# Turning k by a DMA transpose of two 16-bit planes in a recurrence-and-GLU kernel, from the seventh chunk on

## The chip, the cores and the metric

One NeuronCore of one Trainium2 chip runs the kernel in one launch. The metric is the device time of one execution in microseconds, as the median of three runs; beside it stands one execution that the hardware profiler recorded, and all rows below are of that one. The engines are named as the profile names them: PE is TensorE's matmul (PEld its weight load), DVE is VectorE, ACT is ScalarE, POOL is GpSimd, SP is the sync engine, which issues nearly all DMAs here.

## What is computed

A linear recurrence with a decay for each channel, over 4 batches, 8 heads and 768 steps with head size 48, and then a gated linear unit on its 3072 outputs of width 384.

```python
for t in range(S):                                   # per batch and head
    cur = np.einsum('bhd,bhe->bhde', u[None] * kt, vt)
    y[:, :, t] = np.einsum('bhd,bhde->bhe', rt, state + cur)
    state = wt[:, :, :, None] * state + np.einsum('bhd,bhe->bhde', kt, vt)
...
g = x @ w_gate                                       # x: [3072, 384], w_gate: [384, 1536]
silu = g * (1.0 / (1.0 + np.exp(-g)))
val = x @ w_val
return (silu * val @ w_out).astype(np.float32)
```

## The kernel before

The steps are cut into 24 chunks of 128, numbered so that chunk n belongs to batch n mod 4. A chunk's k and r come as one tile `kr` with channels on 112 partitions (two heads of 48 with 16 empty ones between) and four head pairs times 128 steps beside each other. Two scans on DVE (`scan`, `scan2`) run along the decays; `kq` and `re` multiply k and r with them. Within a chunk the recurrence is then three kinds of matmul: `sc` gives the scores of k against r, `dl` the chunk's contribution to the state from k and v, and `y` or, from chunk 6 on, `yy` the outputs from scores, v and state. `dl` needs k with the steps on partitions. `kb` makes it with four TensorE transposes for each chunk into a PSUM buffer (tag `pa`, two buffers, shared with `sc` and `yy`), and `kn` copies that buffer to SBUF on ACT.

From chunk 6 on (`PAIRED = 6`) two chunks n and n + 1 go together through `sc`, `dl` and `yy`, with chunks of 64 steps inside. Their outputs pass through ACT (`xp`), ten small DMAs on SP that move them to the layout of the GLU (`xd`), and a split into a high and a low part (`xh` on ACT, `xl` on DVE).

The GLU runs over seven groups of 4, 2, 4, 4, 4, 4 and 2 chunks' outputs (`GROUPS`). For each group and each of 12 blocks f of 128 hidden channels there are two sets of nine matmuls, `gv` with j = 0 and 1 (PSUM, two buffers), then `silu` (ACT, reads j = 0), `sg` (DVE, multiplies with j = 1), `hh` (ACT) and `hl` (DVE), which split the product, and `po`, three matmuls for each tile of 128 outputs. All products use a high and a low part, hence three matmuls for one. The weights are loaded and split into the two parts during the first group (`raw` to `lower`).

The order of all this is one table, `ORDER`, whose items are run through a dictionary of functions; an item `gv:2:5:1` is group 2, block 5, j = 1, and `kn:13` is kn of chunk 13. Each engine, and SP's queue of DMAs, executes its own instructions in the order of the table, and waits where data or a buffer is missing. `nat` (k and r with steps on partitions, loaded for the diagonal: `ru`, `ruk` and `a0` on DVE use it) lives in a tag with one buffer, `at` in one with three:

```python
nats[n] = ld.tile([P, 2, H, D], F32, tag="nat", name=f"nat_{n}", bufs=1)
...
ats[n, j] = a = ap_.tile([P, 2, NPR, HALF], F32, tag="at", name=f"at_{n}_{j}", bufs=3)
...
for item in ORDER.split():
    name, *at = item.split(":")
    ops[name](*(int(a) if a.isdigit() else a for a in at))
```

Of the kernel before, what the change touches and what calls it, by code (L numbers as in the profile page):

```python
# [70 lines left out]
gv:0:8:1 gv:0:8:0 half spb:5 hh:0:7 pred:5:1 upper:9 y:5 hl:0:7 top:10 xh:5 lower:9 scan:6 kr:7 dl:5  # L71
silu:0:8 low:10 top:11 vt:7 shift:10 po:0:7 low:11 sign:10 sg:0:8 plus:10 hh:0:8 whole:6 a0:6 gv:0:9:1
gv:0:9:0 kr:6 upper:10 hl:0:8 lower:10 po:0:8 xm:5 silu:0:9 sg:0:9 shift:11 sign:11 gv:0:10:0 hh:0:9
nat:7 plus:11 upper:11 hl:0:9 gv:0:10:1 po:0:9 kq:6 silu:0:10 lower:11 sg:0:10 seed:6 scan2:6 vt:6
# [5 lines left out]
hh:1:2 check2:4 vt:8 po:1:1 gv:1:3:0 hl:1:2 silu:1:3 gv:1:3:1 sc:6 sg:1:3 re:8 dl:6 hh:1:3 hl:1:3 st1:6  # L80
st1:7 zs:7:1 ruk:8 ws2:2 ws:9 st2:6 po:1:2 ob:0:3 out:0:3 gv:1:4:0 zero:8 check2:2 st2:7 silu:1:4 scan:9
gv:1:4:1 own:6:0 seed:9 sg:1:4 ob:0:1 zs:7:0 hh:1:4 a0:8 po:1:3 gv:1:5:0 rc:7 pred:6:1 whole:9 zs:6:1
hl:1:4 gv:1:5:1 nat:9 silu:1:5 pred:6:0 sg:1:5 yy:6 kr:10 sps:8 ru:9 gv:1:6:0 kq:9 hh:1:5 gv:1:6:1
po:1:4 scan2:9 hl:1:5 silu:1:6 xp:6:1 sps:9 sg:1:6 ruk:9 hh:1:6 ws:10 hl:1:6 gv:1:7:0 re:9 xp:6:0 zero:9
po:1:5 gv:1:7:1 a0:9 scan:10 silu:1:7 seed:10 sg:1:7 gv:1:8:0 kb:8 nat:10 kb:9 kq:10 ws2:5 hh:1:7
gv:1:8:1 whole:10 hl:1:7 zs:8:0 kn:9 scan2:10 kn:8 po:1:6 silu:1:8 sg:1:8 rc:9 gv:1:9:0 check2:5 hh:1:8
ru:10 gv:1:9:1 out:0:2 own:8:0 sc:8 out:0:1 own:8:1 hl:1:8 xd:6 silu:1:9 ruk:10 sg:1:9 dl:8 st1:8 kr:11
xh:6 st1:9 pred:8:0 po:1:7 hh:1:9 gv:1:10:0 vt:10 pred:8:1 a0:10 st2:8 zs:9:1 zs:8:1 rc:8 st2:9 vt:11
zs:9:0 hl:1:9 yy:8 silu:1:10 nat:11 zero:10 gv:1:10:1 xp:8:1 sg:1:10 re:10 ws:11 ws:12 scan:11 po:1:8
gv:1:11:1 xp:8:0 hh:1:10 whole:11 hl:1:10 kq:11 po:1:9 gv:1:11:0 silu:1:11 kb:11 kb:10 xd:8 ru:11 xl:6  # L90
sg:1:11 hh:1:11 ruk:11 xh:8 hl:1:11 po:1:10 xl:8 po:1:11:c1 kn:10 sps:11 po:1:11:c0 a0:11 seed:11
zs:11:0 scan2:11 gv:2:0:0 gv:2:0:1 re:11 nat:12 ru:12 silu:2:0 zero:11 kr:12 own:10:0 gv:2:1:1 sg:2:0
gv:2:1:0 hh:2:0 scan:12 ob:1:0 seed:12 hl:2:0 silu:2:1 po:2:0:c2 whole:12 sg:2:1 own:10:1 rc:11
po:2:0:c3 kq:12 hh:2:1 gv:2:2:1 gv:2:2:0 scan2:12 ob:1:1 ruk:12 ws2:6 hl:2:1 po:2:0:c0 kn:11 sps:10
check:12 silu:2:2 kr:13 po:2:0:c1 re:12 sc:10 sg:2:2 dl:10 pred:10:0 zero:12 ws:13 st1:10 a0:12 check2:6
st1:11 po:2:1 pred:10:1 vt:12 nat:13 gv:2:3:0 scan:13 hh:2:2 st2:10 st2:11 hl:2:2 vt:13 po:2:2 silu:2:3
ru:13 ruk:13 gv:2:3:1 a0:13 rc:10 zs:10:0 sg:2:3 zs:11:1 gv:2:4:0 gv:2:4:1 seed:13 out:1:1 nat:14 hh:2:3
whole:13 hl:2:3 silu:2:4 gv:2:5:1 zs:10:1 kq:13 sg:2:4 scan2:13 yy:10 xp:10:1 ws:14 ru:14 hh:2:4 hl:2:4
sps:12 kr:14 zero:13 xp:10:0 gv:2:5:0 st2:20 silu:2:5 ruk:14 po:2:3 sg:2:5 kr:15 re:13 gv:2:6:0 hh:2:5
hl:2:5 scan:14 kb:12 kb:13 silu:2:6 gv:2:6:1 sg:2:6 po:2:4 hh:2:6 a0:14 hl:2:6 xd:10 kq:14 gv:2:7:0  # L100
sps:13 whole:14 gv:2:7:1 kn:13 seed:14 silu:2:7 scan2:14 kn:12 sg:2:7 own:12:0 re:14 nat:15 sc:12
check:13 dl:12 po:2:5 st1:12 zero:14 own:12:1 vt:15 st1:13 ws:15 zs:12:0 scan:15 pred:12:0 gv:2:8:0
hh:2:7 kq:15 st2:12 pred:12:1 seed:15 check:14 st2:13 po:2:6 rc:13 ws:16 ru:15 st2:21 whole:15 hl:2:7
po:2:7 ruk:15 gv:2:8:1 zs:13:0 zs:12:1 scan2:15 silu:2:8 re:15 gv:2:9:0 check:15 xh:10 sg:2:8 hh:2:8
ws2:1 zs:13:1 rc:12 hl:2:8 yy:12 sps:14 gv:2:9:1 rc:14 a0:15 silu:2:9 po:2:8 kr:17 out:1:0 own:14:1
xp:12:0 gv:2:10:0 zero:15 check2:1 zs:14:0 sg:2:9 hh:2:9 hl:2:9 gv:2:10:1 vt:17 xp:12:1 xd:12 kr:16
silu:2:10 xh:12 sg:2:10 hh:2:10 scan:16 xl:10 hl:2:10 gv:2:11:1 nat:16 xl:12 gv:2:11:0 kb:14 kb:15 ru:16
po:2:9 own:14:0 silu:2:11 gv:3:0:0 sg:2:11 kn:15 seed:16 sps:15 vt:14 kn:14 hh:2:11 po:2:10 ruk:16
hl:2:11 silu:3:0 vt:16 ws2:3 sc:14 dl:14 po:2:11:c0 st1:14 whole:16 ob:2:0 st1:15 kq:16 po:2:11:c3
st2:14 st2:15 po:2:11:c1 gv:3:0:1 sg:3:0 scan2:16 gv:3:1:0 hh:3:0 po:2:11:c2 check2:3 hl:3:0 a0:16  # L110
out:2:0 ob:2:2 zs:14:1 silu:3:1 pred:14:1 gv:3:1:1 ob:2:1 sg:3:1 re:16 po:3:0:c3 gv:3:2:0 hh:3:1 rc:15
nat:17 po:3:0:c0 zero:16 hl:3:1 out:2:2 gv:3:2:1 po:3:0:c1 ws:17 zs:15:0 ob:2:3 silu:3:2 pred:14:0
zs:15:1 po:3:0:c2 sg:3:2 ru:17 hh:3:2 gv:3:3:0 hl:3:2 po:3:1 yy:14 ruk:17 rc:16 xp:14:0 silu:3:3
gv:3:3:1 gv:3:4:0 sps:16 scan:17 check:16 sg:3:3 gv:3:4:1 a0:17 nat:18 whole:17 po:3:2 ru:18 hh:3:3
hl:3:3 silu:3:4 sg:3:4 hh:3:4 gv:3:5:1 own:16:0 seed:17 ruk:18 hl:3:4 gv:3:5:0 po:3:3 a0:18 kq:17 ws:18
kb:16 xp:14:1 scan2:17 silu:3:5 kb:17 own:16:1 nat:19 gv:3:6:0 vt:19 re:17 sg:3:5 hh:3:5 zero:17
gv:3:6:1 kr:18 po:3:4 hl:3:5 xd:14 silu:3:6 sg:3:6 po:3:5 hh:3:6 kn:17 kn:16 rc:17 gv:3:7:0 scan:18
kq:18 check:17 hl:3:6 whole:18 silu:3:7 sc:16 out:2:3 dl:16 seed:18 sps:17 scan2:18 st1:16 ru:19 st1:17
zs:16:1 zs:17:1 pred:16:1 ws:19 zero:18 re:18 po:3:6 check:18 st2:16 zs:16:0 ws2:8 st2:17 gv:3:7:1
# [842 lines left out]
```

## Time and profile before

| | |
|---|---|
| median of three runs | 562.36 us (560.94 to 563.23) |
| the profiled execution, its own time | 560.63 us |
| its span, first to last instruction | 558.9 us |
| PE busy, share of the span | 545.6 us, 98% |
| DVE busy | 326.1 us, 58% |
| ACT busy | 260.1 us, 47% |
| DMA traffic | 54.64 MB, mean 98 GB/s |

Busy time is counted between the first start and the last end of overlapping instructions. A matmul's end is modelled, and matmuls overlap, so the price of one on TensorE is read from the start of one to the start of the next. The page's chain follows the work that ended last backwards from the end; the timeline lists instructions in order of time with idle time in brackets; the windows give the busy time of each engine by stage.

### The profile page before, as it was taken

Reading aid. Unit: us, or ns where it says so; the run is one execution under the profiler, and the core shown is the slowest. Engines: PE = TensorE matmul, PEld = TensorE weight load, DVE = VectorE, ACT = ScalarE, POOL = GpSimd, SP = SyncE. Lnnn points to the kernel's source line nnn. Section 1 sums busy time; section 2 is a strip of 40 time slices with the busy share of each in tenths; the row PEclk is TensorE's granted clock in tenths of the full one; section 3 lists DMA queues with packets and bytes.
Section 4 is the critical chain, followed back from the end, with each engine's and each line's share of the span. In section 5 each row is a group of like instructions: output and inputs, shape, how many; then the busy total and the mean of one; then the engine's idle time right before and its main releaser. Section 6 shows DMA issues by size and latency. Waiting matters only on the chain.

```text
span 558.9 us, 12807 instructions
## 1 busy us (share of the span) xinstructions
PE 545.6 (98%) x5406; PEld 478.0 (86%) x5406; DVE 326.1 (58%) x523; ACT 260.1 (47%) x535; POOL 4.8 (1%) x36
## 2 busy tenths in 40 slices
...
GB/s 249 276 168 212 129 193 167 225 43 162 103 205 75 109 103 104 68 90 125 74 48 114 71 51 89 42 109 31 113 10 71 87 36 0 1 25 22 15 32 61
DMA packets 28494, 54.64 MB, mean 98 GB/s; under 512 B 4176, under 2 KB 14800, under 8 KB 28432
## 3 DMA queue, kind: packets, MB, share of 16 engines
...
q14 instruction: 18, 0.15, 0.1%
q10 hardware_dynamic: 160, 0.10, 0.1%
...
## 4 chain that ended last, share of the span: by engine, by line
PE 88%; DMA 5%; DVE 2%; SPq 2%; ACT 1%; issue 1%; ACTq 0%; DVEq 0%
PE gv L733 51%; PE po L772 26%; DMA kr<-in_kr_dram 4%; PE y L658 3%; PE sc L516 2%; PE dl L594 2%; PE kb L483 1%; SPq L690 1%; PE y L634 1%; DMA ws<-in_wt_dram 1%; PE sc L505 1%; PE gv_0b L733 0%; PE gv_1b L733 0%; DMA x<-late 0%; SPq L287 0%
## 5 line engine op out<-in xcount | busy, mean ns | idle before, releaser
L733 PE MATMUL gv<-x,w_h 128*128 128x512 f32 (+1 forms) x984 | 285.2, 362 | 2.7 <-ACT x L699 1.7
L733 PEld LDWEIGHTS gv<-x,w_h 128*128 128x128 f32 x984 | 176.6, 188 | 32.9 <-ACT x L699 2.0
L733 PE MATMUL gv<-x,w_l 128*128 128x512 f32 (+1 forms) x492 | 176.8, 359 | 0.0
L746 DVE TENSOR_TENSOR sg<-sg,gv 128x512 f32<-128x512 f32 (+1 forms) x82 | 49.9, 608 | 136.0 <-PE gv L733 101.7
L733 PEld LDWEIGHTS gv<-x,w_l 128*128 128x128 f32 x492 | 92.4, 188 | 12.0
L751 ACT ACTIVATE hh<-sg 128x512 fp32r<-128x512 f32 (+1 forms) x82 | 46.6, 568 | 112.4 <-DVE sg L746 72.1
L772 PE MATMUL po<-w_h,hh 128*128 128x384 f32 x280 | 96.1, 343 | 0.0
L772 PE MATMUL po<-w_h,hl 128*128 128x384 f32 x280 | 94.7, 338 | 0.0
L772 PE MATMUL po<-w_l,hh 128*128 128x384 f32 x280 | 94.1, 336 | 0.0
L743 ACT ACTIVATE sg<-gv 128x512 f32<-128x512 f32 (+1 forms) x82 | 43.7, 532 | 86.7 <-PE gv L733 63.9
L756 DVE TENSOR_TENSOR hl<-sg,hh 128x512 fp32r<-128x512 f32 (+1 forms) x82 | 50.1, 611 | 45.7 <-ACT hh L751 45.0
L772 PEld LDWEIGHTS po<-w_h,hh 128*128 128x128 f32 x280 | 52.5, 188 | 2.9 <-ACT hh L751 0.4
L772 PEld LDWEIGHTS po<-w_h,hl 128*128 128x128 f32 x280 | 52.5, 188 | 2.7 <-DVE hl L756 0.7
L772 PEld LDWEIGHTS po<-w_l,hh 128*128 128x128 f32 x280 | 52.5, 188 | 0.0
L403 DVE TENSOR_TENSOR_SCAN qt<-ws,d 112x516 f32<-112x516 f32 x24 | 29.5, 1228 | 3.8 <-DMA ws<-in_wt_dram 3.8
L419 DVE TENSOR_TENSOR_SCAN et<-ws,d 112x516 f32<-112x516 f32 x24 | 29.5, 1230 | 3.1 <-ACT pend L408 2.3
L794 ACT ACTIVATE ob<-po 128x384 f32<-128x384 f32 x23 | 11.2, 485 | 16.2 <-PE po L772 13.8
L576 ACT ACTIVATE vz<-late 48x192 f32<-48x192 f32 x36 | 12.9, 361 | 10.7 <-DVE late L607 9.3
L434 ACT ACTIVATE ws<-ws,w_top 112x517 f32<-112x517 f32 x24 | 17.5, 730 | 0.8
L315 ACT ACTIVATE w_h<-s 128x1152 fp32r<-128x1152 f32 x12 | 13.9, 1162 | 7.7 <-DVE s L312 7.7
L294 ACT ACTIVATE raw<-raw 128x1152 f32<-128x1152 f32 x12 | 15.4, 1287 | 3.2 <-issue 1.6
L679 ACT ACTIVATE late<-y 112x512 f32<-112x512 f32 x18 | 10.3, 590 | 13.9 <-PE y L658 13.9
...
## 6 DMA issues: line engine op xcount, KB each, us to landing
...
ws<-in_wt_dram SPq DMA_DIRECT2D x36, 226.2 KB, 3.4
kr<-in_kr_dram SPq DMA_DIRECT2D x16, 448.0 KB, 5.5
...
late<-in_kr_dram SPq DMA_DIRECT2D x8, 448.0 KB, 5.0
...
```

The source lines that it names most:

```text
L294: keep(nc.scalar.activation(t, t, AF.Copy, scale=2.0**-112))
L315: keep(nc.scalar.activation(w_h[:, f], ints[f].bitcast(F32), AF.Copy))
L403: keep(nc.vector.tensor_tensor_scan(_flat(qts[n])[:, ::-1], wss[n][:, 1:][:, ::-1], _flat(d1)[:, ::-1], 0.0, ALU.mult, ALU.add))
L419: keep(nc.vector.tensor_tensor_scan(_flat(ets[n]), wss[n][:, :L], _flat(d1), 0.0, ALU.mult, ALU.add))
L434: keep(nc.scalar.activation(w, w, AF.Relu, bias=w_top2, accum_out=over[:, n : n + 1]))
L658: pin(nc.tensor.matmul(ys[n][h][64 * j : 64 * j + m, p, c, :], lhs, rhs, start=first, stop=last,))
L733: pin(nc.tensor.matmul(ps, a[:, f, j, q * P : (q + 1) * P], x[:, q, lo * P : hi * P], start=m == 0, stop=m == 3 * NK - 1,))
L743: keep(nc.scalar.activation(sgs[g, f, h], ps, AF.Silu))
L746: keep(nc.vector.tensor_tensor(sgs[g, f, h], sgs[g, f, h], gvs.pop((g, f, 1, h)), ALU.mult))
L751: keep(nc.scalar.activation(hhs[g, f, h], t, AF.Copy))
L756: keep(nc.vector.tensor_tensor(hls[g, f, h], t, hhs[g, f, h].bitcast(F32), ALU.subtract))
L772: pin(nc.tensor.matmul(pos[g, j], a[:, ts], x[:, f, 2, :], start=f == 0 and i == 0, stop=f == NF - 1 and i == 2,))
```

## The change

From chunk 6 on `kb` is no longer called. `kp` on ACT copies the 32-bit words of k, after `kq`, as 16-bit halves into two planes of 512 elements on each partition, in a buffer of the tag `at`. `kt`, a DMA transpose that SP issues, turns these 1024 columns in eight blocks of 128 into the buffer that `nat` uses, so that the steps are on partitions. `kn` on ACT joins the two planes to 32-bit words again and now reads 896 elements of 16 bits from SBUF in place of 448 words from PSUM. For the first six chunks nothing changes in kind. The table `ORDER` is the same for its first 324 items, up to the eighth block of the first group, and written anew behind them: 18 items `kb` are gone, 18 `kp` and 18 `kt` have come.

```diff
@@ ORDER, one of the lines that differ
-kn:7 re:7 po:0:11:c1 po:0:11:c2 po:1:0:c1 zero:7 ob:0:2 gv:1:2:1 kr:8 sg:1:1 zs:6:0 ru:8 po:1:0:c0
+gv:1:0:1 scan2:7 po:0:11:c0 sg:1:0 kp:7 ob:0:0 re:7 po:0:11:c2 gv:1:1:0 kt:6 ob:0:2 hh:1:0 gv:1:1:1
...
@@ -486,13 +487,37 @@
                     kbs[n][:, p, PR : PR + 2], prods[n][:, p, :], u_head[:, :, p], start=True, stop=True,
                 ))
 
+    kps, kts = {}, {}
+
+    def kp(n):
+
+        t = ap_.tile([P, 2, NPR, HALF], F32, tag="at", name=f"kp_{n}", bufs=3)[:PR]
+        t = t.rearrange("d c p t -> d (c p t)")[:, : NPR * C].bitcast(U16)
+        k = _flat(krs[n][:, 0]).bitcast(U16)
+        keep(nc.scalar.activation(
+            t.rearrange("d (i x) -> d i x", i=2), k.rearrange("d (x i) -> d i x", i=2), AF.Copy,
+        ))
+        kps[n] = t
+
+    def kt(n):
+
+        t = ld.tile([P, 2, H, D], F32, tag="nat", name=f"kt_{n}", bufs=1)
+        t = t.rearrange("s i h e -> s (i h e)")[:, : NPR * PR].bitcast(U16)
+        kts[n] = t.rearrange("s (g d) -> s g d", g=2 * NPR)
+        keep(nc.sync.dma_start_transpose(kts[n], kps.pop(n)))
+
     def kn(n):
         if n >= PAIRED and n % 2:
             kns[n] = late("kn").rearrange("s (p d) -> s p d", p=NPR)
         else:
             kns[n] = ap_.tile([P, NPR, PR + 2], F32, tag="kn", name=f"kn_{n}", bufs=1)
-        lo, hi = 0, PR + 2 if n < SUMMED else PR
-        keep(nc.scalar.activation(kns[n][:, :, lo:hi], kbs.pop(n)[:, :, lo:hi], AF.Copy))
+        if n < PAIRED:
+            keep(nc.scalar.activation(kns[n], kbs.pop(n)[:, :, : PR + 2], AF.Copy))
+        else:
+            keep(nc.scalar.activation(
+                kns[n][:, :, :PR].bitcast(U16).rearrange("s p (d i) -> s i p d", i=2),
+                kts.pop(n).rearrange("s (i p) d -> s i p d", i=2), AF.Copy,
+            ))
 
     def sc(n):
```

On PE, in the second group's last block, eight transposes stood between the end of one gv and a po of the block before. In the names, `gv_11_0` is block 11 with j = 0, `x_1` the group's input and kb the PSUM tile that takes the turned k. Before:

```order
L733 MATMUL gv_11_0_2303<-x_1_988,w_h 128x256
L733 MATMUL gv_11_0_2303<-x_1_988,w_l 128x256
L733 MATMUL gv_11_0_2303<-x_1_1052,w_h 128x256
L483 MATMUL kb_2315<-ident,kr_2144 128x112 x4
L483 MATMUL kb_2320<-ident,kr_1885 128x112 x4
L772 MATMUL po_0_1579<-w_h,hh_10_2291 128x384
```

After, the same gv is followed by the next gv:

```order
L758 MATMUL gv_11_0_2288<-x_1_988,w_h 128x256
L758 MATMUL gv_11_0_2288<-x_1_988,w_l 128x256
L758 MATMUL gv_11_0_2288<-x_1_1052,w_h 128x256
L758 MATMUL gv_11_1_2318<-x_1_988,w_h 128x256
L758 MATMUL gv_11_1_2318<-x_1_988,w_l 128x256
L758 MATMUL gv_11_1_2318<-x_1_1052,w_h 128x256
```

The two rows of four transposes each are gone; in the whole program eighteen such rows are.

On ACT, around chunks 12 and 13, which lie in the third group. `late` is a shared area that here holds the odd chunk's kn, `sg_7` is written by silu of block 7, `vz` by zs. Before, the two kn read the PSUM tiles kb:

```order
L751 ACTIVATE hh_5_2799<-sg_5_2770 128x512
L743 ACTIVATE sg_6_2815<-gv_6_0_2789 128x512
L751 ACTIVATE hh_6_2840<-sg_6_2815 128x512
L408 ACTIVATE pend<-qt_2803 112x4
L495 ACTIVATE late_1444<-kb_2810 128x448
L743 ACTIVATE sg_7_2882<-gv_7_0_2858 128x512
L495 ACTIVATE kn_2886<-kb_2805 128x4x112
L433 ACTIVATE ws_2560<-ws_2560 112x517
L434 ACTIVATE ws_2560,over<-ws_2560,w_top_108 112x517
L576 ACTIVATE vz_99<-late_1444 48x192
```

After (kp of chunks 14 and 13 in this order, then kn of 13 and of 14, which read the transposed tiles kt):

```order
L497 ACTIVATE kp_2865<-kr_2770 112x1024
L776 ACTIVATE hh_6_2870<-sg_6_2837 128x512
L497 ACTIVATE kp_2876<-late_1461 112x1024
L768 ACTIVATE sg_7_2890<-gv_7_0_2855 128x512
L601 ACTIVATE vz_101<-late_1462 48x192
L517 ACTIVATE late_1462<-kt_2892 128x2x448
L776 ACTIVATE hh_7_2945<-sg_7_2890 128x512
L768 ACTIVATE sg_8_3018<-gv_8_0_3006 128x512
L601 ACTIVATE vz_101<-late_1462 48x192
L601 ACTIVATE vz_99<-late_1462 48x192
L517 ACTIVATE kn_3036<-kt_3021 128x2x4x112
```

Two copies have come in front, and each kn now waits for a DMA; behind the kn of chunk 13 stand hh of block 7 and silu of block 8.

On SP, behind the ten copies of x of chunks 10 and 11 (the last of them is the first row here). Before:

```order
L690 DMA x_3_2846<-late_1445 48x256 x2
L388 DMA nat_2892<-in_nat_dram 128x768
L395 DMA vt_2980<-in_vn_dram 128x384
L377 DMA ws_2983<-in_wt_dram 112x517
L377 DMA ws_3022<-in_wt_dram 112x517
L377 DMA ws_3075<-in_wt_dram 112x517
L384 DMA late_1443<-in_kr_dram 112x1024
L810 DMA out_dram<-ob_0_2420 128x384
L395 DMA late_1444<-in_vn_dram 128x384
```

After:

```order
L715 DMA x_3_2804<-late_1463 48x256 x2
L396 DMA vt_2815<-in_vn_dram 128x384
L378 DMA ws_2819<-in_wt_dram 112x517
L389 DMA nat_2823<-in_nat_dram 128x768
L396 DMA vt_2872<-in_vn_dram 128x384
L507 DMA_TRANSPOSE kt_2892<-kp_2876 128x8x112
L835 DMA out_dram<-ob_0_2418 128x384
L507 DMA_TRANSPOSE kt_3021<-kp_2865 128x8x112
L389 DMA nat_3059<-in_nat_dram 128x768
```

Two transposes stand in the queue now, between loads; the nat behind the second one uses the buffer that it fills.

## Rows read from the trace of the kernel before

**Rows 1.** Page, part 1: busy us, share of the span, instructions.

```profile
PE 545.6 (98%) x5406; PEld 478.0 (86%) x5406; DVE 326.1 (58%) x523; ACT 260.1 (47%) x535; POOL 4.8 (1%) x36
```

**Rows 2.** Page, part 4: chain that ended last, by engine and by line.

```profile
PE 88%; DMA 5%; DVE 2%; SPq 2%; ACT 1%; issue 1%; ACTq 0%; DVEq 0%
PE gv L733 51%; PE po L772 26%; DMA kr<-in_kr_dram 4%; PE y L658 3%; PE sc L516 2%; PE dl L594 2%; PE kb L483 1%; SPq L690 1%; PE y L634 1%; DMA ws<-in_wt_dram 1%; PE sc L505 1%; PE gv_0b L733 0%; PE gv_1b L733 0%; DMA x<-late 0%; SPq L287 0%
```

**Rows 3.** Timeline, PE: start us, us, instruction, count; chunks 8 and 9.

```profile
153.73 0.28 PE L733 MATMUL gv<-x,w_h 128*128 128x256 f32 x1
153.85 0.93 PE L483 MATMUL kb<-ident,late 112*128 112x112 f32 x8
154.55 0.36 PE L733 MATMUL gv<-x,w_h 128*128 128x256 f32 x1
```

**Rows 4.** Line 483 (kb): count, ns min/median/max, first and last start.

```profile
L483 PE MATMUL kb<-ident,kr x64: 257/259/316, 6.5 to 458.2; 112*128 112x112 f32 x64
...
L483 PE MATMUL kb<-ident,late x32: 257/259/262, 153.8 to 394.4; 112*128 112x112 f32 x32
```

**Rows 5.** Timeline, PE: nine gv, then 24 po, four tiles wide.

```profile
231.18 0.39 PE L733 MATMUL gv<-x,w_h 128*128 128x512 f32 x1
...
233.25 0.34 PE L772 MATMUL po<-w_h,hh 128*128 128x384 f32 x1
...
237.41 0.39 PE L733 MATMUL gv<-x,w_h 128*128 128x512 f32 x1
```

**Rows 6.** Timeline, PE: nine gv of the second group, two tiles wide.

```profile
168.84 0.28 PE L733 MATMUL gv<-x,w_h 128*128 128x256 f32 x1
...
169.90 0.34 PE L772 MATMUL po<-w_h,hh 128*128 128x384 f32 x1
```

**Rows 7.** ACT by form: busy us, mean ns, idle before.

```profile
L315 ACT ACTIVATE w_h<-s 128x1152 fp32r<-128x1152 f32 x12 | 13.9, 1162 | 7.7 <-DVE s L312 7.7
...
L699 ACT ACTIVATE x<-x 128x768 fp32r<-128x768 f32 x9 | 7.6, 839 | 11.6 <-DMA x<-late 11.6
L495 ACT ACTIVATE kn<-kb 128x448 f32<-128x448 f32 x9 | 4.9, 540 | 0.9 <-PE kb L483 0.9
```

**Rows 8.** DMA issues by line: count, KB each, median us to landing.

```profile
ws<-in_wt_dram SPq DMA_DIRECT2D x36, 226.2 KB, 3.4
kr<-in_kr_dram SPq DMA_DIRECT2D x16, 448.0 KB, 5.5
...
x<-late SPq DMA_DIRECT2D x54, 48.0 KB, 2.0
```

**Rows 9.** Timeline, SP: issue of ten copies of x.

```profile
153.83 6.44 SPq L690 DMA_DIRECT2D x<-late  x10
...
167.86 6.96 SPq L690 DMA_DIRECT2D x<-late  x10
```

**Rows 10.** Timeline, ACT: xp of chunks 8 and 9.

```profile
166.75 1.09 ACT L679 ACTIVATE late<-y 112x512 f32<-112x512 f32 x2 [0.69 <-PE y L658]
```

**Rows 11.** Timeline, PE: start of the third group, idle in brackets.

```profile
172.02 0.96 PE L483 MATMUL kb<-ident,kr 112*128 112x112 f32 x8
...
175.35 0.34 PE L772 MATMUL po<-w_l,hh 128*128 128x384 f32 x1
177.38 0.50 PE L733 MATMUL gv<-x,w_h 128*128 128x512 f32 x1 [1.70 <-ACT x L699]
...
178.38 0.50 PE L733 MATMUL gv<-x,w_h 128*128 128x512 f32 x1 [0.26 <-DVE x L711]
```

**Rows 12.** Windows: busy us (count) by engine, PEclk, DMA share, GB/s.

```profile
100.00:160.00 60.00, 60.00 (x723) 56.62 (x714) 51.07 (x86) 32.18 (x69) 0.53 (x5) 1.00 0.46 136
160.00:240.00 80.00, 77.20 (x928) 67.26 (x920) 51.89 (x92) 33.17 (x73) 0.53 (x5) 1.00 0.34 104
...
400.00:480.00 80.00, 80.00 (x677) 69.67 (x676) 33.66 (x55) 27.98 (x56) 0.11 (x1) 1.00 0.18 50
```

More of the change, by code (lines that the diff above doesn't have):

```diff
@@ L70 @@
 gv:0:7:1 raw:10 ruk:6 hl:0:6 pred:5:0 silu:0:7 lower:8 shift:9 low:9 sg:0:7 sign:9 po:0:6 plus:9 raw:11
[L71 to L74, printed above, removed]
@@ L80 @@
[L80 to L84, printed above, removed]
@@ L85 @@
[L85 to L119, printed above, removed]
@@ new lines @@
+whole:6 lower:10 gv:0:9:0 silu:0:9 po:0:8 sg:0:9 shift:11 half gv:0:10:1 hh:0:9 kr:6 sign:11 kr:7
+plus:11 upper:11 gv:0:10:0 hl:0:9 po:0:9 silu:0:10 xh:5 kq:6 lower:11 seed:6 scan2:6 xm:5 sg:0:10 re:6
+hh:0:10 kp:6 nat:7 ru:7 zero:6 st:5 gv:0:11:0 ws2:4 check2:4 hl:0:10 gv:0:11:1 silu:0:11 scan:7 ruk:7
+xl:5 po:0:10 room kr:8 a0:7 kr:9 seed:7 whole:7 gv:1:0:0 sg:0:11 hh:0:11 kq:7 hl:0:11 silu:1:0 ws:8
+gv:1:0:1 scan2:7 po:0:11:c0 sg:1:0 kp:7 ob:0:0 re:7 po:0:11:c2 gv:1:1:0 kt:6 ob:0:2 hh:1:0 gv:1:1:1
@@ new lines @@
+hl:1:8 silu:1:9 rc:8 ruk:10 gv:1:9:1 zero:10 sg:1:9 kp:10 pred:8:1 dl:8 a0:10 ws:11 st1:8 zs:8:1 st1:9
+re:10 st2:8 xd:6 zs:9:1 yy:8 nat:11 po:1:7 xp:8:0 po:1:8 ws:12 xp:8:1 scan:11 st2:9 ru:11 kr:12 hh:1:9
+xh:6 kq:11 whole:11 hl:1:9 gv:1:10:1 gv:1:10:0 ruk:11 xl:6 silu:1:10 sg:1:10 vt:10 po:1:9 gv:1:11:0
+seed:11 out:0:3 hh:1:10 a0:11 xd:8 hl:1:10 scan2:11 re:11 gv:1:11:1 st2:22 silu:1:11 po:1:10 sg:1:11
+sc:10 hh:1:11 xh:8 hl:1:11 zero:11 po:1:11:c1 kt:10 po:1:11:c0 xl:8 scan:12 seed:12 kq:12 own:10:1
@@ new lines @@
+zs:13:0 re:14 kn:13 hh:2:7 dl:12 po:2:6 zero:14 hl:2:7 st1:12 scan:15 st1:13 own:12:0 kq:15 st2:12
+st2:13 seed:15 gv:2:8:0 pred:12:0 out:1:0 silu:2:8 zs:13:1 kt:14 gv:2:8:1 pred:12:1 zs:12:1 sg:2:8 kn:14
+gv:2:9:1 gv:2:9:0 whole:15 nat:15 scan2:15 rc:12 hh:2:8 hl:2:8 zs:12:0 ws:16 ru:15 silu:2:9 yy:12
+gv:2:10:1 xp:12:0 po:2:7 ruk:15 xp:12:1 sps:15 sg:2:9 check:15 hh:2:9 hl:2:9 gv:2:10:0 zero:15 po:2:8
+re:15 silu:2:10 gv:2:11:0 kr:16 kp:15 scan:16 a0:15 xd:12 kq:16 sg:2:10 kt:15 xh:12 own:14:1 sps:14
```

119 lines of the change are left out of this document (75 added, 44 removed).

## The prediction

> **What bounds the kernel now.** I read the page's shares first, then the chain, then the stages, then the places where TensorE waits. TensorE is busy 545.6 of 558.9 us, ScalarE 260.1 us, VectorE 326.1 us [rows 1]; the chain that ended last is 88% TensorE, and gv and po of the GLU alone are 77% of the span [rows 2]. The granted clock is 1.00 of full speed in every stage, so 2.4 GHz [rows 12]. So from about 100 us on the end is set by the sum of TensorE's instructions, and an edit gains what it takes from that sum, less what it makes TensorE wait. VectorE is the next engine in the stage from 100 to 160 us, busy 51 of 60 us; ScalarE has 32 there, and in the last stage both are idle more than half the time [rows 12].
>
> **Taken from TensorE.** A pair of chunks turns k by eight transposes. They start at 153.85 us and the next matmul starts at 154.55 us, so eight cost 0.70 us, whatever their modelled ends say [rows 3]. The 96 transposes of the trace [rows 4] are 24 of the first six chunks, which stay, and 72 of the other eighteen, which go: nine blocks of eight, 9 x 0.70 = 6.3 us. Each block stands between matmuls that follow without a gap, so it comes off the end in full unless a wait takes its place. The order confirms that no such row is left behind the sixth chunk. The PSUM buffers (two, shared with sc and yy) are asked for less often; no wait in the rows is theirs, so I count nothing for that.
>
> **Given to ScalarE.** kp copies 1024 16-bit elements on 112 partitions, kn now 896 instead of 448. Rows by form: 448 elements 0.54 us, 768 elements 0.84, 1152 elements 1.16 [rows 7]; between the last two 1024 elements come to about 1.05 us, and 896 to 0.95, that is 0.41 more than now. Whether 16-bit elements with a stride of two go at that price no row shows; by elements it is the upper end, by bytes (half as many) the lower end would be 0.6 us. I take the upper. Eighteen times 1.46 us is 26 us, on an engine with 299 us of idle time [rows 1]: in the densest stage about four or five chunks fall into 28 idle us [rows 12], so 7 us of work. I cost it at nothing on the path. The cover is that idle time; where a copy stands ahead of a silu or hh that TensorE needs, it costs up to 1.05 us once, and such cases are in the next term.
>
> **The new wait: kn behind the transfer.** kt is issued by SP and moves 224 KB; kn waits for its landing, and ScalarE works in order, so behind kn wait the silu and hh of the current block, and dl waits for kn itself. The trace has no such transfer. The nearest rows: a load of the same 226 KB lands after 3.4 us, a load of 448 KB after 5.5 us, an SBUF-to-SBUF copy of 48 KB after 2.0 us [rows 8]; the far upper end is the other change of layout by DMA in this kernel, the ten copies of x, which need 7 us to be issued and 2 us more to land [rows 9, 8]. I take 3.4 us, the row of the same size.
>
> What that costs follows from where kt and kn stand. In units of TensorE's own work (nine gv matmuls 2.07 us, a tile of po three matmuls 0.52 us [rows 5]; in the second group with its half tiles 1.06 us [rows 6]) the new order puts between kt and kn of chunks 6 to 23: 2.1, 2.1, 1.1, 5.0, 4.7, 8.8, 4.1, 2.8, 2.1, 4.2, 5.2, 4.1, 4.2, 5.2, 2.1, 0, 0 and 4.1 us. If ScalarE is held longer than that, TensorE still has one gv tile to do before it needs the next silu: 1.06 us for chunks 6 to 9, 2.07 after them. Only for 7, 13 and 21 dl follows at once, 2.1, 2.8 and 0.7 us of work behind kt, and there kn's own 0.95 us counts too.
>
> With 3.4 us from each kt's written place this gives 0.2 + 2.2 + 1.3 (chunks 6 to 8) + 1.5 (13) + 3.6 + 1.3 (21, 22) = 10.2 us, which would be more than the change takes away. But SP runs ahead of the written place: the ten copies for chunk 8 stand in the old order behind kb of chunks 10 and 11, which ran at 172.02 us [rows 11], and were issued from 167.86 us on [rows 9], 4.2 us ahead. The transposes depend on two engines (kp, and the last reader of the one buffer that nat and kt share), so I allow them half, 2 us. A landing that is late by 1.4 us instead of 3.4 costs 0.2 us at chunk 7 and 1.6 us at 21, and nothing elsewhere: 1.9 us. That is my term; 10.2 us and zero are its ends.
>
> The Trainium skill has a figure for the transfer itself: the page "DMA: Bandwidth & Descriptors", section "Latency and other measured facts", gives 261 GB/s for a DMA transpose with a gap in the middle dimension. As an estimate from that page 224 KB would move in 0.9 us, and with the 2.0 us of the small copy the landing would be 2.9 us; the term would then be 1.2 us, at chunk 21 alone. No run here shows it, and my sum does not use it.
>
> **SP's queue.** kt is one more issue for each of eighteen chunks, among loads that have their data long before they are used, and behind it wait nat of the next chunk and, for the even chunks, the ten copies of x. Ten copies hold SP for 6.4 to 7.0 us [rows 9], 0.6 to 0.7 us each; if one kt costs SP one to two of these, eighteen cost it 13 to 25 us out of the whole span, and nothing of that is on the path except before a group's first gv.
>
> **The order anew: one wait that may go.** The third group's first gv waits for the x of chunks 8 and 9: po ends its issue at 175.35 us, gv starts at 177.38 us and is held again until 178.38 us, together 2.3 us lost, with the copies of x released by ScalarE's xp, which ends at 167.84 us [rows 9 to 11]. From xp to that gv the chain takes 177.38 - 167.84 = 9.5 us. The old order has 4.9 us of TensorE work between them, the new one 8.2 us, because the pair's yy stands earlier. So up to 2.3 us come back, if the longer way through kp, kt and kn doesn't make yy late. I take half, 1.2 us.
>
> **The sum.** The profiled execution took 560.6 us (span 558.9 us): 560.6 - 6.3 - 1.2 + 1.9 = 555.0 us. The three runs have a median of 562.4 us, 1.7 us above the profiled one, so 556.7 us.
>
> **Rivals.**
>
> Rival 1, the gain is eaten: 6.3 + 1.2 us are balanced when the landing is late by 2.9 us, since chunks 7, 8, 13, 21 and 22 then cost 7.5 us (1.7 + 0.8 + 1.0 + 3.1 + 0.8); with SP 2 us ahead that is a landing of 4.9 us. For it: loads in the queue ahead of kt delay it, as kr's 5.5 us shows [rows 8], and VectorE, which makes the data for kp and frees the buffer, is busy 85% of the stage of chunks 6 to 9 [rows 12]. Against: the DMA engines, busy 0.46 of the time from 100 to 160 us, are down to 0.18 from 400 us on [rows 12]. Time about 562 us, between 559.5 and 565.
>
> Rival 2, slower, one mechanism: the landing is slow for every chunk, and ScalarE stands before kn. It decides from a landing of 5.4 us on, where it costs over 2.8 us net; at 7 us (late by 5) the same list gives 21.5 us, so 560.6 - 7.5 + 21.5 + 1.7 = 576 us. For it speaks that the two changes of layout known from this trace differ by far from a plain copy: x needs 9 us for 384 KB [rows 8, 9]. Against: that is ten issues at 0.6 us, and kt is one. The Trainium skill speaks against this change here: the page "VectorE: DVE Perf Modes", section "The three transpose paths", gives 1309 ns for a 128x128 transposition by DMA against 390 ns on TensorE, and its rules prefer TensorE if PSUM will do as the destination. If the eight blocks of a kt went one after another at that price, the landing would be 10.5 us as an estimate from that page, and by the same list the time some 622 us; if they overlap as the packets of a load do, nothing of it follows. The TensorE side already disagrees with the trace, 0.09 us each in a row [rows 3].
>
> Rival 3, the change does nothing: TensorE is not what ends, and the 6.3 us turn into waits for x of the next group, whose chain through VectorE (scans, products) is untouched. Against: apart from the 2.3 us above TensorE waits for little [rows 12]: from 160 to 240 us, with that gap in it, it is busy 77.2 of 80 us, from 400 to 480 us all 80.0. Time 560 to 563 us.
>
> **How the numbers follow.** My forecast, the landing below 4.4 us and the order keeping its promise: 0.62, 553 to 559.5 us. Better than 553 us: 0.03. Rival 1: 0.19, of it 0.02 over the upper bound of no change. Rival 2: 0.13. Rival 3: 0.03. A measurement of this kernel tells about 0.5% (2.8 us) from no change. So faster 0.65, same 0.20, slower 0.15. The range: the low end is all 2.3 us regained and no new wait, 560.6 - 6.3 - 2.3 + 1.7 = 553.7, rounded down to 553 for the freed PSUM buffers; the high end is the full 10.2 us with nothing regained, 566.2. That leaves out rival 2 and what is better than 553, some 0.16.
>
> **What would show it.** Right: no transposes after the sixth chunk and TensorE's busy time down by 6 us; kt landing in 2.5 to 4.5 us; kn waiting under 2 us in most chunks, with dl of chunks 12 and 20 the ones that wait; ScalarE at about 286 us; the gap at the third group's first gv gone or halved. Wrong: ScalarE idle before kn for more than 40 us in sum, TensorE idle "until ACT" in every block that follows a kn, or kt holding SP for several microseconds so that nat or x come late. A landing over 5.4 us alone would turn the sign.

## The result, and the profile after

The changed kernel takes 557.31 us (median of 15 runs, 552.11 to 560.34), the kernel before 561.32 us beside it (15 runs, 558.60 to 563.67): a ratio of 0.9917, 95% interval 0.9889 to 0.9946. (The ratio is the one on record, and not the quotient of the two medians, which is 0.9929; all comparisons below go by such ratios.) The median is 0.6 us above the forecast, which started from a base 1.0 us higher (562.4 us), and on the side that it gave the best chance. That the number came so close is luck: two terms of the forecast were off by more than the noise, in opposite directions, and their errors cancelled in good part; the experiments show how.

The profiled execution after has a span of 556.2 us. The page's shares and chain (parts 1 and 4), to be set beside [rows 1] and [rows 2], and three windows (busy us and count by engine, PEclk, DMA share, GB/s), beside [rows 12]:

```profile
PE 539.0 (97%) x5331; PEld 471.2 (85%) x5334; DVE 326.0 (59%) x523; ACT 288.3 (52%) x553; POOL 4.7 (1%) x36
...
PE 66%; DMA 13%; DVE 9%; ACT 7%; SPq 3%; issue 2%; DVEq 0%; ACTq 0%
```

```profile
100.00:160.00 60.00, 58.85 (x729) 54.15 (x729) 50.34 (x85) 38.01 (x73) 0.42 (x4) 1.00 0.61 158
160.00:240.00 80.00, 77.00 (x914) 66.42 (x915) 52.20 (x93) 41.20 (x79) 0.53 (x5) 1.00 0.44 113
...
400.00:480.00 80.00, 80.00 (x674) 70.09 (x674) 32.02 (x53) 32.15 (x61) 0.10 (x1) 1.00 0.18 48
```

TensorE's busy time fell by 6.6 us, ScalarE's rose by 28.2. The chain runs through TensorE for 66% where it was 88%, but most of that is not the change's: ahead of 115 us, where the first group's weights are loaded and split and no kt has been issued yet, TensorE's part of the chain is 4 us instead of 79, and in the kernel with one more buffer (below) it is 79 us again. Behind 115 us it fell from 413 to 361 us, and there the chain passes through kt, kn and the load of nat at 141, 206 and 322 us. From 100 to 160 us TensorE is no longer busy all the time (58.85 of 60), and the stage from 160 to 240 us, which held the third group's gap, is as it was (77.00, before 77.20).

The new instructions by line (L507 is kt, L517 kn, L497 kp; count, ns min/median/max, first and last start), and how long kt takes to land:

```profile
L507 SPq DMA_TRANSPOSE kt<-kp x18: 1222/1230/1345, 123.6 to 463.1; - x18
...
DMA to landing us min/median/max: 2.9/2.9/4.5
...
L517 ACT ACTIVATE kn<-kt x9: 1224/1237/1257, 129.1 to 461.9; 128x896 uint16<-128x896 uint16 x9
...
  DMA kt<-kp: 7.1, 6
...
L497 ACT ACTIVATE kp<-kr x10: 1040/1049/1057, 119.8 to 455.8; 112x1024 uint16<-112x1024 uint16 x10
```

The transfer lands after 2.9 us, and ScalarE stood idle before kn for 7.1 us in all, in six places. So the wait that the prediction looked at is small. What TensorE waited for, and VectorE for nat (waits: us in total, times, longest), in the kernel after:

```profile
PE gv L758 <- ACT x L724: 1.3, 1, 1.3
...
PE gv L758 <- ACT sg L768: 1.0, 1, 1.0
PE dl L619 <- ACT late L517: 0.9, 1, 0.9
...
PE gv L758 <- DVE sg L771: 0.6, 1, 0.6
...
DVE nat L455 <- DMA nat<-in_nat_dram: 11.5, 6, 5.2
```

Only the 0.9 us of dl are kn's (`late` here is the odd chunk's kn). The last row was "6.7, 4, 3.0" in the trace of before (there it is line 454): VectorE waits longer for nat, a load that the change doesn't touch. That was the lead. From each of TensorE's instructions behind 100 us to the next one's start, summed by kind, before and after: kb 6.3 and 0, gv 266.9 and 267.7, po 141.4 and 141.9, y 19.3 and 20.1, dl 10.1 and 10.9, sc 8.8 and 9.2 us. The transposes took their 6.3 us with them, and all that is left grew by 3.3 us. Of these, 1.8 us lie ahead of the second group's first gv (it starts at 123.73 us, before at 121.93), where single traces of one kernel differ by more (121.73 and 125.07 us in two of the kernel with the buffer of its own, below).

### The profile page after: what moved, and what is told of

Same layout as the page of the kernel before. It is cut to its first block, busy times and chain, and to the rows that moved or that the text cites. A ratio compares the mean times of both kernels' runs of the same rounds, so it can differ in the third digit from the quotient of the medians.

```text
span 556.2 us, 12705 instructions
## 1 busy us (share of the span) xinstructions
PE 539.0 (97%) x5331; PEld 471.2 (85%) x5334; DVE 326.0 (59%) x523; ACT 288.3 (52%) x553; POOL 4.7 (1%) x36
## 2 busy tenths in 40 slices
DMA packets 45199, 58.78 MB, mean 106 GB/s; under 512 B 20880, under 2 KB 31504, under 8 KB 45136
## 4 chain that ended last, share of the span: by engine, by line
PE 66%; DMA 13%; DVE 9%; ACT 7%; SPq 3%; issue 2%; DVEq 0%; ACTq 0%
PE gv L758 40%; PE po L797 21%; DMA kr<-in_kr_dram 5%; DMA raw<-in_wo_dram 3%; DMA nat<-in_nat_dram 2%; SPq L715 2%; DMA kt<-kp 2%; PE y L683 2%; DVE s L313 1%; DVE s L309 1%; DMA x<-late 1%; PE dl L619 1%; PE sc L541 1%; DVE w_l L319 1%; ACT w_h L316 1%
## 5 line engine op out<-in xcount | busy, mean ns | idle before, releaser
L771 DVE TENSOR_TENSOR sg<-sg,gv 128x512 f32<-128x512 f32 (+1 forms) x82 | 49.7, 607 | 123.7 <-PE gv L758 93.3
L300 ACT ACTIVATE raw<-raw 128x1152 int32<-128x1152 uint32 x12 | 15.5, 1293 | 6.7 <-DMA raw<-in_wo_dram 6.7
L434 ACT ACTIVATE ws<-ws 112x517 f32<-112x517 f32 x24 | 15.1, 629 | 7.3 <-DMA ws<-in_wt_dram 4.8
```

Source lines behind the costliest of these rows:

```text
L300: keep(nc.scalar.activation(t, t.bitcast(U32), AF.Copy, scale=2.0**-29))
L771: keep(nc.vector.tensor_tensor(sgs[g, f, h], sgs[g, f, h], gvs.pop((g, f, 1, h)), ALU.mult))
```

## The experiments

Differences below are the ratio's distance from 1 times the 561.2 us of before.

**What the transposes are worth in the old order.** The kernel before; from chunk 6 on the transposes are left out and kn copies a constant, so k is not turned.

```diff
     def kb(n):
+        if n >= PAIRED:
+            return
...
     def kn(n):
+        if n >= PAIRED:
+            src = w_h[:, 0, :2].rearrange("s c d -> s (c d)").bitcast(F32)[:, : NPR * PR]
+            keep(nc.scalar.activation(kns[n][:, :, :PR], src.rearrange("s (p d) -> s p d", p=NPR), AF.Copy))
+            return
```

> The old order without the 72 transposes: from chunk 6 on kb is left out and kn copies 448 elements of a constant from SBUF, so k is not turned at all. This is the term of 6.3 us by itself, with no transfer, no kp and no new order. Theory (TensorE's sum sets the end): 6.3 us under the kernel before, a ratio of 0.989, about 555 us beside 561.3. Rival (the gain of the change comes from the new order, and the transposes were hidden by other waits): within 2 us of the kernel before, a ratio over 0.996.

556.51 us (9 runs), ratio 0.9933 (0.9905 to 0.9961): 3.8 us less, not 6.3. The third group's start in its timeline on PE (idle in brackets):

```profile
176.93 0.50 PE L739 MATMUL gv<-x,w_h 128*128 128x512 f32 x1 [1.42 <-ACT x L705]
177.93 0.50 PE L739 MATMUL gv<-x,w_h 128*128 128x512 f32 x1 [0.26 <-DVE x L717]
```

The gap of [rows 11] is still there: the blocks of transposes before it went, the x chain did not move. So in the old order some of what is taken from TensorE turns into waits, as rival 3 had it for all of it: by the sums from start to start kb's 6.3 us are gone, but po takes 143.6 us instead of 141.4.

**The order alone, twice.** The new order with kb and kn of TensorE in it. First with both chunks' kb and kn right ahead of the pair's first sc or dl:

> The new order with the turn left on TensorE: kp and kt are taken out, and kb and kn of both chunks of a pair stand ahead of the first sc or dl of the pair. Theory (the order alone brings nothing): the 6.3 us are back, ratio to the kernel before 0.998 to 1.006, 560 to 564.5 us. Rival (the new order is the gain): ratio about 0.992, 557 us, as the changed kernel.

560.08 us (12 runs), ratio 0.9987 (0.9966 to 1.0008). That looks as if the order were worth nothing. But the trace has eight waits of sc for kn, and by the sums from start to start kb and sc took 7.9 us more than before while gv, po, y and dl took 8.3 us less. This placing had hidden the order's gain. So again, with the transposes up to two GLU steps earlier (chunks 16 and 17 as an example):

```diff
-own:16:0 gv:3:8:1 gv:3:8:0 silu:3:8 po:3:6 sg:3:8 kb:16 kb:17 kn:16 kn:17
+own:16:0 gv:3:8:1 kb:16 kb:17 kn:16 kn:17 gv:3:8:0 silu:3:8 po:3:6 sg:3:8
```

> The new order with k of all chunks still turned by TensorE; the eight transposes of both chunks of a pair stand up to two GLU steps ahead of the pair's first sc or dl, so that sc doesn't stand right behind kn. In the earlier run of this kind sc waited eight times for kn, kb and sc took 7.9 us more than before, and gv, po, y and dl together took 8.3 us less. Theory (the new order by itself takes several us of small waits out of gv and po): 555 to 557 us, ratio 0.990 to 0.993. Rival (the new order is worth at most the 1.2 us of the prediction): 559.5 us or more, ratio 0.997 or more.

557.03 us (11 runs), ratio 0.9931 (0.9910 to 0.9953): 3.9 us from the order by itself, with the transposes placed like this, and no wait of gv is left among TensorE's waits. The prediction gave the order 1.2 us.

**The new order without any turning.** The changed kernel without kp and kt; kn copies a constant, so k is not turned here either.

> The new order without any turning of k from the seventh chunk on: kn copies a constant of 448 words, so the output is not the reference's. There is no transpose on TensorE, no transfer, no shared buffer. Theory (turning by TensorE 6.3 us, order about 5 us; what the changed kernel loses to the buffer that kt and nat share is the rest): 548.5 to 550.5 us, ratio 0.977 to 0.982, the same as the kernel with a buffer of its own within 2 us. Rival (the order is worth 1.2 us at most, and the kernel with its own buffer is fast for another reason): 553 to 555 us, ratio 0.986 to 0.990.

548.82 us (6 runs), ratio 0.9803 (0.9769 to 0.9837). Beside the kernel above the turning on TensorE costs 1.28% or 7.2 us in this order; with intervals of 1.2 and 1.9 us on the two that agrees with the 6.3 us of [rows 3, 4]. The changed kernel, at 0.9917, is 6.4 us slower than this one: that is what its way of turning costs. Beside the old order without turning (0.9933) the new order is worth 7.3 us, and with the transposes in it 3.9: the two gains are not independent of each other.

**A buffer of its own for kt.** In the changed kernel kt fills the one buffer of `nat`. Here it gets a place of its own; the two small state tiles that lay there go into an array that is free from chunk 6 on.

```diff
     def kt(n):
-        t = ld.tile([P, 2, H, D], F32, tag="nat", name=f"kt_{n}", bufs=1)
-        t = t.rearrange("s i h e -> s (i h e)")[:, : NPR * PR].bitcast(U16)
+        t = late("kt").bitcast(U16)
...
-            befores[n] = late(f"ta{n % 2}")[:PR].rearrange("d (p e) -> d p e", p=NPR)
+            h = n % 2 * NPR * D
+            befores[n] = _flat(sp)[:, h : h + NPR * D].rearrange("d (p e) -> d p e", p=NPR)
```

> The changed kernel with one edit: the transposed tile gets a buffer of its own, so that the load of nat for the next chunk no longer waits for kn. In the trace of after VectorE stands 11.5 us before ru for that load, and TensorE's gaps at 212 and 335 us follow from it. Theory (a part of the gain is given back by the shared buffer): those two gaps of 0.8 and 1.2 us go, 1 to 2.5 us less than the changed kernel, about 555.5 us, ratio 0.987 to 0.990. Rival (what is given back is ScalarE's load and the landing): the time of the changed kernel, ratio 0.991 to 0.993.

550.25 us (6 runs), ratio 0.9820 (0.9781 to 0.9858), 5 us better than expected. That the two state tiles moved as well is not the reason: the kernel without any turning leaves them where they were and is as fast. It computes everything and beats both kernels; a second run of it follows below. Its waits for nat, and TensorE's longest waits behind the front:

```profile
PE dl L619 <- ACT late L516: 0.9, 1, 0.9
PE gv L758 <- DVE x L736: 0.4, 2, 0.3
...
DVE nat L455 <- DMA nat<-in_nat_dram: 0.8, 2, 0.5
```

VectorE's waits for nat fell from 11.5 to 0.8 us. The gain lies in two stretches. From the second group's first gv to the third group's it is 55.3 us in the changed kernel (123.73 to 179.05), and 52.3, 53.1 and 53.4 us in the traces of this run, of its repeat and of the kernel with a swap (both at the end of this section); from there to the end it is 377.2 us against 374.6, 375.5 and 374.8. How the sharing reached TensorE is to be seen in the changed kernel at about 206 us (timeline: start us, us, instruction, idle in brackets):

```profile
206.20 1.24 ACT L517 ACTIVATE kn<-kt 128x896 uint16<-128x896 uint16 x1
...
207.47 0.33 SPq L389 DMA_DIRECT2D nat<-in_nat_dram  x1
...
211.70 0.56 DVE L455 TENSOR_TENSOR nat<-nat,u_bc 128x384 f32<-128x384 f32 x1 [5.18 <-DMA nat<-in_nat_dram]
212.17 0.68 DVE L771 TENSOR_TENSOR sg<-sg,gv 128x512 f32<-128x512 f32 x1
...
212.91 0.50 PE L758 MATMUL gv<-x,w_h 128*128 128x512 f32 x1 [0.62 <-DVE sg L771]
```

kn ends at 207.44, nat's load is issued 0.03 us later, VectorE, in order, stands 5.18 us before it, and sg, which frees the PSUM buffer that gv needs, is late behind it. The other way is SP's queue, ahead of the third group. In the changed kernel (first fence) and with the buffer of its own (second), the timeline of SP, ACT and PE:

```profile
153.36 1.22 SPq L507 DMA_TRANSPOSE kt<-kp  x1
157.54 0.35 SPq L389 DMA_DIRECT2D nat<-in_nat_dram  x1
158.42 6.99 SPq L715 DMA_DIRECT2D x<-late  x10
...
168.71 1.09 ACT L704 ACTIVATE late<-y 112x512 f32<-112x512 f32 x2 [3.35 <-DMA x<-late]
...
169.82 6.86 SPq L715 DMA_DIRECT2D x<-late  x10
...
179.05 0.50 PE L758 MATMUL gv<-x,w_h 128*128 128x512 f32 x1 [1.29 <-ACT x L724]
```

```profile
149.16 1.69 SPq L506 DMA_TRANSPOSE late<-kp  x1
151.57 0.38 SPq L389 DMA_DIRECT2D nat<-in_nat_dram  x1
152.51 7.04 SPq L715 DMA_DIRECT2D x<-late  x10
164.78 6.84 SPq L715 DMA_DIRECT2D x<-late  x10
...
174.00 0.50 PE L758 MATMUL gv<-x,w_h 128*128 128x512 f32 x1
```

From kt to nat it is 4.2 us in the first and 2.4 in the second; the ten copies stand behind nat, ScalarE's xp of the next chunks waits 3.35 us for these to land, the next ten copies follow it, and the gap of 1.29 us is at the group's start again. That this gap is the buffer's is not shown, however. The same gv in the kernel without any turning, in the repeat with the buffer of its own, and in the kernel with the swap:

```profile
171.52 0.50 PE L754 MATMUL gv<-x,w_h 128*128 128x512 f32 x1 [1.02 <-ACT x L720]
...
178.17 0.50 PE L758 MATMUL gv<-x,w_h 128*128 128x512 f32 x1 [0.30 <-ACT x L724]
...
175.22 0.50 PE L758 MATMUL gv<-x,w_h 128*128 128x512 f32 x1 [0.88 <-ACT x L724]
```

The gap comes and goes without a shared buffer; the two stretches above do not. The sharing also holds kt back for the readers of the nat before. What SP's queue waited for in the changed kernel (`a` is the last of nat's readers):

```profile
SPq L507 <- DVE a L464: 21.7, 5, 15.2
...
SPq L389 <- ACT kn L517: 12.8, 5, 5.5
...
SPq L389 <- DMA kt<-kp: 7.1, 5, 3.3
```

With the buffer of its own none of the three is left. So both directions are there, and the run takes away both and doesn't tell them apart. Nor does it single out the clock: the median granted clock of the runs is 0.995 in the changed kernel and 0.998 with the buffer of its own, which on 556 us would be some 1.7 us of the difference (an estimate, for a TensorE that always has work).

**Is it the queue?** The changed kernel with its shared buffer; the ten copies for chunks 6 and 7 (`xd:6`) stand ahead of nat of chunk 10.

```diff
-sg:1:8 nat:10 gv:1:9:0
+sg:1:8 xd:6 nat:10 gv:1:9:0
...
-re:10 st2:8 xd:6 zs:9:1
+re:10 st2:8 zs:9:1
```

> The changed kernel, shared buffer and all, with one item of the order moved: the ten copies of x of chunks 6 and 7 stand ahead of the load of nat of chunk 10 in SP's queue, not behind it. In the changed kernel's trace that load waits for kn of chunk 9 in the shared buffer and is issued at 157.54 us, the copies from 158.42 us on, the next ten from 169.82 us on, and the third group's first gv waits 1.29 us at 179.05 us for their x. Theory (the load that waits holds the queue, and this is how the shared buffer reaches TensorE there): the copies start about 3 us earlier, the next ten about as much, and the 1.29 us at the third group go; nat of chunk 10 is loaded about 4 us later, which may cost some of it again; 555 to 557 us, ratio 0.988 to 0.992. Rival (x is late for another reason): the third group's wait stays within 0.3 us of 1.29.

559.61 us (12 runs), ratio 0.9957 (0.9929 to 0.9985): not the gain that the theory had, but 2.2 us more than the changed kernel on the ratios, whose intervals overlap a little. The wait at the third group is gone, as expected, but a larger one stands in its place (timeline of SP and DVE, then TensorE's longest wait):

```profile
151.09 6.33 SPq L715 DMA_DIRECT2D x<-late  x10
157.52 1.49 SPq L389 DMA_DIRECT2D nat<-in_nat_dram  x1
...
161.91 0.56 DVE L455 TENSOR_TENSOR nat<-nat,u_bc 128x384 f32<-128x384 f32 x1 [4.67 <-DMA nat<-in_nat_dram]
```

```profile
PE dl L619 <- ACT sg L768: 5.0, 1, 5.0
```

VectorE's hl stands behind nat, ScalarE's sg behind hl, and dl behind sg. The granted clock is at 0.50 from 162.0 to 168.5 us, so the pause costs more than its 5.0 us. So the theory's mechanism holds at that place and its time was missed: in both orders tried, the one of nat and x that stands second is late. Another buffer mends it.

**An exchange in place.** The old order, kt with its own buffer, kp where kb stood, kt behind it, and for each pair kn of the first chunk, kt and kn of the second close together.

```diff
-scan:14 kb:12 kb:13 silu:2:6
+scan:14 kp:12 kp:13 kt:12 silu:2:6
...
-whole:14 gv:2:7:1 kn:13 seed:14 silu:2:7 scan2:14 kn:12 sg:2:7
+whole:14 gv:2:7:1 kn:12 kt:13 seed:14 silu:2:7 scan2:14 kn:13 sg:2:7
```

> The old order with the turn by DMA: kp stands where kb stood, kt of a pair's first chunk right behind, kn of the first and kt of the second where the first kn stood, and kt has a buffer of its own. From the first kt to the end of the second kn the trace of after has 2.9 + 1.2 + 2.9 + 1.2 = 8.2 us, with 5.3 us of TensorE work for the second pair and 7.4 to 9.4 for four others. Theory (the order had to make room for the landing): ScalarE held twice for each pair for 2 to 3 us, some 6 us of new waits, so 559 to 564 us, ratio 0.996 to 1.005. Rival (the landing is hidden anyway): ratio 0.989 to 0.992, 555 to 557 us.

604.91 us (6 runs), ratio 1.0787 (1.0754 to 1.0820), 40 us over what I expected. The first pair in its timeline (SP, ACT, PE), and windows with the granted clock (PEclk, the third number from the right):

```profile
127.66 5.52 SPq L506 DMA_TRANSPOSE late<-kp  x2
...
130.71 1.22 ACT L516 ACTIVATE kn<-late 128x896 uint16<-128x896 uint16 x1 [2.81 <-DMA late<-kp]
134.88 1.20 ACT L516 ACTIVATE late<-late 128x896 uint16<-128x896 uint16 x1 [2.95 <-DMA late<-kp]
...
136.46 0.69 PE L797 MATMUL po<-w_h,hh 128*128 128x384 f32 x1 [6.64 <-ACT ob L819]
```

```profile
134.00:138.00 4.00, 1.54 (x5) 1.54 (x6) 0.00 (x0) 2.40 (x5) 0.00 (x0) 0.50 0.97 222
138.00:142.00 4.00, 3.69 (x21) 3.28 (x20) 3.51 (x7) 0.39 (x1) 0.11 (x1) 0.73 0.78 178
142.00:146.00 4.00, 4.00 (x144) 3.81 (x143) 1.99 (x6) 2.45 (x6) 0.00 (x0) 1.00 0.43 120
```

Two transfers through one buffer run one after the other with kn between them; ScalarE waits 2.81 and 2.95 us, the po that need its ob stand 6.64 us. Behind the pause TensorE runs at 0.50, its 1.2 GHz level, and is back at 2.4 GHz by 142 us. This is rival 2's mechanism with a landing of only 2.9 us: what should make the transfer harmless in the changed kernel is the distance that the new order puts between kt and kn. That it is this distance alone is argued and not shown, as the run has the rest of the old order too.

**A slower transfer.** In the changed kernel each kt is issued three times.

```diff
-        keep(nc.sync.dma_start_transpose(kts[n], kps.pop(n)))
+        for _ in range(3):
+            keep(nc.sync.dma_start_transpose(kts[n], kps[n]))
+        kps.pop(n)
```

> The changed kernel with each transfer kt issued three times. One issue holds SP for 1.23 us, so kn's data and the release of the shared buffer come about 2.5 us later in each of the eighteen chunks. Theory (kn's data is a little late at two chunks now, and nat's load, which follows kn in the shared buffer, moves by the same 2.5 us): by the list of the prediction a landing late by 3.9 us instead of 1.4 costs 10 us more, and nat's part comes on top: 567 to 575 us. Rival (there is slack behind kt that the list doesn't see): 558 to 561 us.

633.70 us (4 runs), ratio 1.1311 (1.1265 to 1.1358). The edit was larger than I wrote: each repeat waits for the landing of the one before, so kn's data come at least 3 x 2.9 = 8.7 us behind the first issue (10.5 in the first two rows here), 5.8 us or more later than in the changed kernel.

```profile
119.07 8.84 SPq L508 DMA_TRANSPOSE kt<-kp  x3
...
129.62 1.22 ACT L519 ACTIVATE kn<-kt 128x896 uint16<-128x896 uint16 x1 [4.97 <-DMA kt<-kp]
...
147.05 0.99 PE L621 MATMUL dl<-vt,late 64*64 64x48 f32 x30 [5.56 <-ACT late L519]
```

By the prediction's list of distances a landing late by 8.7 us costs 71 us, and with SP 2 us ahead 38; measured are 78 us over the changed kernel. The list counts waits alone, though. Of the 72.6 us between the two traces' spans, TensorE is idle for 49.7 more (66.9 beside 17.2) and busy for 22.9 more (561.9 beside 539.0) with the same matmuls, at a mean granted clock of 0.954 beside 0.998. So the waits lie between the list's two numbers, the later nat among them, and that 71 comes close to the whole is partly chance. It is steep all the same: nothing to speak of at 2.9 us, 14% at 8.7 and more.

**Is ScalarE's work free?** In the changed kernel each kp is done twice, 18.8 us more of ScalarE.

```diff
-        keep(nc.scalar.activation(
-            t.rearrange("d (i x) -> d i x", i=2), k.rearrange("d (x i) -> d i x", i=2), AF.Copy,
-        ))
+        for _ in range(2):
+            keep(nc.scalar.activation(
+                t.rearrange("d (i x) -> d i x", i=2), k.rearrange("d (x i) -> d i x", i=2), AF.Copy,
+            ))
```

> The changed kernel with kp done twice: ScalarE has 19 us more, and each kt is issued 1.05 us later. The prediction costed ScalarE's 26 us of new work at nothing. Theory (idle time of ScalarE covers it): the 1.05 us later landing alone costs something, 1 to 4 us, so 558 to 561 us. Rival (ScalarE's copies are on the path at many chunks): 565 us or more.

559.93 us (10 runs), ratio 0.9967 (0.9939 to 0.9995): 2.8 us over the changed kernel on the ratios, with intervals that overlap a little. Its dl waited for kn 2.2 us in two places, where it had waited 0.9 in one. So one kp more costs some 0.15 us, not its 1.05, and the later kt is in that; nearly free, not free.

**One swap on top of the buffer.** With the buffer of its own, kn of chunk 7 ahead of kp of chunk 8 on ScalarE, and the kernel without the swap once more beside it.

```diff
-po:1:2 silu:1:4 kp:8 kn:7 sg:1:4
+po:1:2 silu:1:4 kn:7 kp:8 sg:1:4
```

> The kernel in which kt has a buffer of its own, and one swap in the order: kn of chunk 7 stands ahead of kp of chunk 8 on ScalarE. In the trace of the kernel with its own buffer the transfer for chunk 7 is issued at 128.0 us, kp of chunk 8 runs from 137.1 us, kn of chunk 7 behind it from 138.0 us, and dl waits 0.9 us for it. Theory (that wait is kp's, not the transfer's): the 0.9 us go, so about 1 us less than the same kernel without the swap, ratio to before 0.979 to 0.982, and no wait of dl for kn is left there. Rival (the transfer is what dl waits for): the wait stays, no change.

> The kernel in which kt has a buffer of its own, once more and beside the one with the swap, for a closer comparison: 549 to 552 us, ratio 0.979 to 0.985, under the changed kernel's 0.992 by 6 to 7 us.

550.74 us (5 runs), ratio 0.9826 (0.9799 to 0.9852), and 550.63 us (6 runs), 0.9820 (0.9792 to 0.9847): no difference, and the 1 us looked for is less than the intervals can show. In the trace with the swap the wait of dl for kn is gone, but these are on its list (waits of TensorE):

```profile
PE gv L758 <- ACT x L724: 0.9, 1, 0.9
PE dl L619 <- ACT sg L768: 0.5, 1, 0.5
```

So the wait was kp's, as the theory had it. Whether it moved on to these two is not shown: the first of them is the gap at the third group, which comes and goes. The buffer's gain was there again.

## Why the prediction came out right

TensorE's sum sets the end, as the prediction had it, and the time came out close to the forecast because two errors cancelled. The four kernels in a row give the terms, each with all before it in place; they add up to the measured ratio because each is the difference of two of them.

| term | forecast, us | measured, us | from |
|---|---|---|---|
| order anew | -1.2 | -3.9 | 1 to 0.9931 |
| transposes off TensorE | -6.3 | -7.2 | 0.9931 to 0.9803 |
| transfer, its wait and ScalarE's copies | +1.9 | +1.0 | 0.9803 to 0.9820 |
| one buffer for kt and nat, SP's queue behind it | 0 | +5.4 | 0.9820 to 0.9917 |
| sum | -5.6 | -4.7 | |

The intervals of the single terms are 1.2 to 2.9 us wide to either side, so the first and the last differ from the forecast, the middle two agree with it. How the first 11.1 us split into the two upper rows hangs on where the transposes stand: with them right ahead of sc the order's row would be -0.7.

**Taken from TensorE: right.** The sum from start to start lost exactly the 6.3 us of kb. What the prediction didn't see is how much of this gain needs the new order: in the old one it is 3.8 us.

**Given to ScalarE: right on the whole, wrong in one size.** 288.3 us busy against 286 forecast. kp is 1.05 us as taken from the rows by elements. kn is 1.23, not 0.95: 896 halves that are written two apart cost more than the line through [rows 7] says; whether reading or writing does it, no run tells. That it costs nothing on the path holds but for about 0.15 us, as far as the price of one kp more tells.

**The wait of kn: right in size, wrong in place.** The landing is 2.9 us; I took 3.4. The Trainium skill's page "DMA: Bandwidth & Descriptors", section "Latency and other measured facts", with its 261 GB/s for a DMA transpose and the 2.0 us of the small copy, had given 2.9 us as an estimate. The trace agrees with that sum; no run measures its two parts. The forecast had waits at chunks 7 and 21; there is one, 0.9 us at chunk 7, and that is kp of chunk 8 standing ahead of kn, as the swap shows for the kernel with the buffer of its own. dl of chunks 12 and 20, which I named as the ones to wait, did not.

**SP's queue: the step that failed.** The prediction's "nothing of that is on the path except before a group's first gv" counted kt's issue time alone, and its sum has no term for it. The section on the change says that kt and nat use one buffer and that nat stands behind kt in the queue; the prediction used this only for the lead of SP. The row to read was nat's load: it now waits for kn, which waits for kt, and only then takes its 4.2 us to come to VectorE (207.47 to 211.70), with everything behind it on VectorE and on SP late. 5.4 us, with 2.7 to either side, costed at zero. That the buffer costs this is shown by the runs with and without it; how much of it goes by way of VectorE, of SP's queue, of a later kt and of the clock is not.

**The order anew: under-sized, and then hidden.** I priced one gap of 2.3 us at half. The order by itself brings 3.9 us. In its trace that gap is gone, and many small waits with it: by the sums from start to start gv takes 264.4 us instead of 266.9 and po 138.9 instead of 141.4. In the changed kernel the gap is back, 1.29 and 0.26 us against 1.70 and 0.26 in [rows 11], neither gone nor halved. The copies of x stand behind the late nat there; but as kernels without a shared buffer have up to 1.02 us at the same place, its cause stays open.

**The rivals.** Rival 1 (the gain eaten) is in part what happened, by the buffer and not by the landing. Rival 2 did not come true here, but the exchange in place and the slower transfer, 7.9% and 13.1% slower, show that its mechanism is real. Its price of 10.5 us for a kt from the Trainium skill's page "VectorE: DVE Perf Modes", section "The three transpose paths" (1309 ns eight times), is an estimate that the trace contradicts: the eight blocks of 112 x 128 land together after 2.9 us.
